# Windowed attention and a mixture of adapters: token order restored by the exp's write, the residual added outside TensorE

## The chip, the cores and the metric

The kernel runs on one core of a Trainium2 chip. The metric is the device time of one execution in microseconds (us). The profile shows the core's engines side by side: PE (TensorE, the matrix engine; PEld is its loading of weights), DVE (VectorE), ACT (ScalarE), POOL (GpSimd) and SP (SyncE, which here only issues DMA transfers). SBUF is the on-chip working memory, PSUM the memory that TensorE writes its products to.

## The reference

The first part is attention with a symmetric window of 32 positions, for 8 batches, 8 heads, 576 tokens and a head size of 64. The second part adds to each token a mixture of two of eight adapters of rank 16; both results are summed.

```python
scores = q @ k.T / sqrt(64)             # masked to |i - j| <= 32
attn = softmax(scores); x = attn @ v    # x becomes [4608 tokens, 512]
logits = x @ w_gate                     # 8 experts
top 2 of the logits, w = softmax over these two
delta = sum over the two of w * ((x @ A[e]) @ B[e])
out = x + delta                         # float32
```

The last line is what the change touches: `x` is the residual.

## The kernel before

**Attention.** q and k come in as 9 tiles (t = 0 to 8) of 128 rows, cast from float32 to float16 by DMA transfers that GpSimd issues (`load`, L397). TensorE transposes them (`trans_full`, L482; `trans`, L496 for tile 0), VectorE copies q out of PSUM to `qT` (L505) and ScalarE copies k to `kT`, permuted (L507). A row of a tile holds 16 tokens, so the 128 columns of a score block stand in the order (h, r, s), with two halves h, 16 places r within a row and 4 rows s. The natural order of the tokens is (h, s, r). `score` (L552 writes the mask with matmuls, L564 the scores) fills a PSUM tile `W`, and `expo` (L572) on ScalarE writes the exponentials as float16 into `PT`. 36 such steps run in all. v comes in through 256-byte rows on SyncE's queue (L404), and GpSimd casts it into `vbd` (L462). `pv` (L615; L643 for the last batch) multiplies `PT` with `vbd`, which has a column of ones for the softmax's sum, and VectorE divides (L628, L629; L654, L656) and writes `xs`, the attention's output x in float16.

**Adapters.** For each batch b, five groups g of 128 tokens: TensorE transposes x (`moe_xT`, L708), VectorE copies it out (L713), TensorE multiplies by the adapters' A and the gate (`moe_zl`, L726), the gate is worked out by small operations (`gate1`, `gate_e`, `gate2`, `gate3`, L748 to L769), the gated z is transposed back (`moe_zT`, L776) and copied out by ScalarE (`moe_ez`, L781). This copy also puts the tokens into natural order. `moe_pd` then makes two matmuls for each group into the same PSUM tile: z times B (L794), and x times a permuted identity `po_` (L796), which both adds the residual and brings it into natural order. ScalarE copies the sum to `ob` (`moe_eo`, L803) and SyncE's queue stores it (`moe_st`, L809 and L814). The five groups of a batch are handled in three steps j: groups 0 and 1, groups 2 and 3, group 4. The last batch (`FINE`, `GM`) runs through its gates step by step rather than in one piece.

**The order of the work.** Each piece of work is a task with an engine, an assumed duration, a due time, its predecessors and the buffers that it takes and gives back. `Planner.run` plays these through and so fixes, at build time, one order for each engine. `LEAN` holds an offset of the due time for each kind of task. Each engine executes its instructions in that order and waits in place where an input or a buffer is missing. The pools that matter here are PSUM (`W`, four tiles of 1024 float32, or eight halves `H`), `xs` (4), `ob` (7), `vraw` (5) and `raw` (3 each for q and k). The stores of batch 0 and 1 are planned behind the loads of v for batch 6 and 7.

Of the kernel before, what the change touches and what calls it, by code (L numbers as in the profile page):

```python
# [10 lines left out]
F16 = mybir.dt.float16  # L11
# [12 lines left out]
class Planner:  # L24
# [3 lines left out]
    LAT = 0.1  # L28
    PELAT = 0.26
    STICK = 0.3  # L30
    LEAN = {"cv": 219.41, "cvb": 272.89, "cw": -85.24, "cz": 71.26, "ek": 86.6,
            "eo": 453.57, "eoz": 19.28, "eq": 36.82, "ex": -18.16, "exx": -411.27,
            "exxz": 157.95, "ez": -28.43, "ezz": -32.76, "g1": -34.69, "g1z": 30.3,
            "g2": 61.29, "g2z": -68.02, "g3": -26.85, "g3z": 51.71, "ge": -5.86,
            "gez": -29.31, "ident": 1.61, "ld": -29.04, "ldw": 40.85, "lv": 308.15,
            "mask": 0.64, "nm": 38.08, "nmg": -75.15, "pad": 22.65, "pd": 378.9,
            "pdz": -55.48, "perm": -12.35, "pv": -58.89, "pvg": 96.18, "sc": 366.94,
            "st": 7.28, "stz": -11.9, "tr": -62.44, "wm": 304.62, "xT": -482.21,
            "xTz": 2.47, "zT": 16.38, "zTz": -100.13, "zero": 16.41, "zl": 329.66}
    SWITCH = 0.095  # L40
    BOOT = {"POOL": 1.3, "SP": 0.8, "ACT": 2.1, "DVE": 0.9, "PE": 0.8}
    ROT = 5
    LINE = 128
# [172 lines left out]
def kernel(  # L216
# [31 lines left out]
    QW = NI + 2 * PADQ  # L248
    BI = NP * SL
    SPLIT = (0,)  # L250
    GM = (B - 1,)
    FINE = (B - 1,)
    GATE = {t: [f"cv{t - 2}.0.0"] for t in range(3, NTI)}
# [27 lines left out]
    H = [W[i // 2][:, 512 * (i % 2):512 * (i % 2) + 512] for i in range(2 * NW)]  # L281

    ident = const.tile([128, 128], F16, name="ident")
    po_ = const.tile([128, 128], F16, name="po_")
    mask = const.tile([128, 2, RR, 4], F16, name="mask")
    WA_sb = const.tile([128, NP, ER + E], F16, name="WA")
    B_sb = const.tile([128, DD], F16, name="Bsb")
# [18 lines left out]
    def slot(p, key):  # L306
        return place[p, key]

    def wslot(key):
        return slot("W", key) // 2  # L310
# [27 lines left out]
    def c_ident():  # L338
        make_identity(nc, ident)

    def c_perm():
        nc.gpsimd.tensor_copy(
            out=po_.rearrange("p (h s r) -> p h s r", h=2, s=4),
            in_=ident.rearrange("p (h r s) -> p h s r", h=2, s=4))

    def c_mask():
        nc.gpsimd.memset(mask, 0.0)
        for h in range(2):
# [29 lines left out]
    if PACE:  # L378
        P.add("pace", "SP", 0.1, -20, c_pace, [PACE])
    P.add("ident", "POOL", 0.6, -22, c_ident, ["ld0.0.0"], lat=0.3)  # L380
    P.add("perm", "POOL", 0.3, 0, c_perm, ["ident"])
    P.add("mask", "POOL", 2.6, -21, c_mask, ["ld0.0.1"], lat=0.3)
    P.add("pad", "DVE", 0.3, -10, c_pad)
    for i in range(NVB):
# [184 lines left out]
                        start=False, stop=(i == 3))  # L569

    def expo(t):
        nc.scalar.activation(out=PTs[slot("PT", t)].rearrange("p e i c -> p (e i c)"),  # L572
                             in_=W[wslot(("s", t))],
                             func=AF.Exp, scale=1.0 / float(D) ** 0.5)

    def blocks(t):
# [125 lines left out]
    def moe_xT(b, j):  # L702
        x = xs[slot("xs", b)]
        tp = H16[slot("H", ("x", b, j))]
        for m, g in enumerate(GG[j]):
            for c in range(NP):
                o = 512 * m + 128 * c
                nc.tensor.matmul(out=tp[:, o:o + 128], lhsT=x[:, g].rearrange("p (k c) -> p c k", c=4)[:, c],  # L708
                                 rhs=ident, is_transpose=True, start=True, stop=True)
# [61 lines left out]
    def moe_zT(b, k, g0, g1):  # L771
        zs = zss[b % 2].rearrange("p g e r -> p g (e r)")
        tp = H16[slot("H", ("y", b, k))]
        for g in range(g0, g1):
            o = 128 * (g - g0)
            nc.tensor.matmul(out=tp[:, o:o + 128], lhsT=zs[:, g],  # L776
                             rhs=ident, is_transpose=True, start=True, stop=True)

    def moe_ez(b, k, g0, g1):
        tp = H16[slot("H", ("y", b, k))][:, 0:128 * (g1 - g0)]  # L780
        nc.scalar.copy(  # L781
            out=zTs[b % 2][:, g0:g1].rearrange("p g (h s r) -> p (g h) s r", h=2, s=4),
            in_=tp.rearrange("p (g r s) -> p g s r", r=RR, s=4))

    def pdt(b, j):
        key = ("d", b, j)
        t = H[slot("H", key)] if len(GG[j]) == 1 else W[wslot(key)]
        return t.rearrange("p (i c) -> p i c", c=DD)

    def moe_pd(b, j):  # L790
        pd = pdt(b, j)
        x = xs[slot("xs", b)]
        for i, g in enumerate(GG[j]):
            nc.tensor.matmul(out=pd[:, i], lhsT=zTs[b % 2][:, g], rhs=B_sb,  # L794
                             start=True, stop=False)
            nc.tensor.matmul(out=pd[:, i], lhsT=po_,  # L796
                             rhs=x[:, g],
                             start=False, stop=True)

    def moe_eo(b, j):  # L800
        n = len(GG[j])
        pd = pdt(b, j)
        nc.scalar.copy(out=obs[slot("ob", (b, j))][:, 0:n], in_=pd[:, 0:n])  # L803

    def moe_st(b, j):
        ob = obs[slot("ob", (b, j))]
# [9 lines left out]
    for b in range(B):  # L816
        d0 = 4 * b + 4.6
        fine = b in FINE
        z_ = "z" if fine else ""
        old = b >= 2  # L820
        chunks = [(g[0], g[-1] + 1) for g in GG] if fine else [(0, NG)]
        kold = range(len(GG)) if b - 2 in FINE else range(1)
        for j in range(3):
            n = len(GG[j])
            P.add(f"xT{z_}{b}.{j}", "PE", 0.225 * n, d0 + 0.1 * j, lambda b=b, j=j: moe_xT(b, j),
                  ([f"nmg{b}.{g}" for g in GG[j]] if b in GM else [f"nm{u}" for u in range(4 * b, 4 * b + 4)])
                  + ([f"zl{b - 2}.{k_}" for k_ in kold] if old else []),
                  take=[("H", ("x", b, j))], mode="full", ni=4 * n)
            P.add(f"exx{z_}{b}.{j}", "DVE", 0.15 + 0.27 * n, d0 + 0.1 * j - 0.5, lambda b=b, j=j: moe_ex(b, j),
                  [f"xT{z_}{b}.{j}"], drop=[("H", ("x", b, j))])  # L830
        for k_, (g0, g1) in enumerate(chunks):
            n = g1 - g0
            arg = (b, k_, g0, g1)
            zb = ("W" if n > 2 else "H", ("z", b, k_))
            zn = f"{z_}{b}.{k_}"
            P.add(f"zl{b}.{k_}", "PE", 0.24 * n, d0 + 0.5, lambda arg=arg: moe_zl(*arg),
                  ([f"exx{z_}{b}.{k_}"] if fine else [f"exx{b}.{j}" for j in range(3)]) + ["cw"],
                  take=[zb], mode="full", ni=4 * n)
            if not fine:
                P.add(f"cz{zn}", "ACT", 0.75, d0 - 1, lambda arg=arg: copy_z(*arg), [f"zl{b}.{k_}"]  # L840
                      + ([f"g3{b - 2}.{j}" for j in kold] if old else []), drop=[zb])
            P.add(f"g1{zn}", "DVE", 0.45 if n > 2 else 0.37, d0 - 1, lambda arg=arg: gate1(*arg),
                  [f"zl{b}.{k_}" if fine else f"cz{zn}"]
                  + ([f"zT{b - 2}.{j}" for j in kold] if old else []))
            P.add(f"ge{zn}", "ACT", 0.22, d0 - 1, lambda arg=arg: gate_e(*arg), [f"g1{zn}"])
            P.add(f"g2{zn}", "DVE", 1.0 if n > 2 else 0.88, d0 - 1, lambda arg=arg: gate2(*arg), [f"ge{zn}"])
            P.add(f"g3{zn}", "DVE", 0.33 + 0.15 * n, d0 - 1,
                  lambda arg=arg: gate3(*arg), [f"g2{zn}"], drop=[zb] if fine else [])
            P.add(f"zT{zn}", "PE", 0.055 * n, d0 + 0.8, lambda arg=arg: moe_zT(*arg), [f"g3{zn}"],
                  take=[("H", ("y", b, k_))], mode="full", ni=n)  # L850
            P.add(f"ez{zn}", "ACT", 0.2 + 0.1 * n, d0 + 0.5, lambda arg=arg: moe_ez(*arg),
                  [f"zT{zn}"] + ([f"pd{'z' if b - 2 in FINE else ''}{b - 2}.2"] if old else []),
                  drop=[("H", ("y", b, k_))])
        for j in range(3):
            n = len(GG[j])
            k_ = j if fine else 0
            P.add(f"pd{z_}{b}.{j}", "PE", 0.43 * n, d0 + 1.2 + 0.7 * j, lambda b=b, j=j: moe_pd(b, j),
                  [f"ez{z_}{b}.{k_}", "perm"], soft=[f"pd{z_}{b}.{j - 1}"] if j else [],
                  take=[(PB[n], ("d", b, j)), ("ob", (b, j))], drop=[("xs", b)] if j == 2 else [],
                  mode="full", ni=2 * n)  # L860
            P.add(f"eo{z_}{b}.{j}", "ACT", 0.2 + 0.42 * n, d0 + 1.2 + 0.7 * j,
                  lambda b=b, j=j: moe_eo(b, j), [f"pd{z_}{b}.{j}"],
                  drop=[(PB[n], ("d", b, j))])
            P.add(f"st{z_}{b}.{j}", "SP", 0.38 * (2 if j == 0 else 1), d0, lambda b=b, j=j: moe_st(b, j),
                  [f"eo{z_}{b}.{j}"], lat=1.2,
                  soft=[f"lv{b + HOLD}.1.1"] if b + HOLD < B else [])
            P.add(f"ds{b}.{j}", "Q1", 0.7 * n, d0, None, [f"st{z_}{b}.{j}"],
                  drop=[("ob", (b, j))], lat=0.8, pkt=88.0)
# [41 lines left out]
```

The softmax here doesn't subtract the row's maximum and nothing guards it: scores larger than these inputs give would overflow.

## Time and profile before

| | |
|---|---|
| time, median of 3 runs | 147.33 us (143.87 to 149.73) |
| profiled execution | 144.49 us, span 142.6 us |
| TensorE, VectorE, ScalarE, GpSimd busy | 116.4, 94.0, 84.7, 63.7 us |
| residual matmuls (L796) | 40, 10 of them before and 30 after 98.6 us |
| input read, output written | 28.85 MB, 9.44 MB |

Busy time is the time in which an engine's record shows an instruction; a matmul's end is modelled, so that the starts of successive matmuls say more than their durations. A line of the profile names the kernel's line, the engine, the operation, what it writes and reads, the shape and the count. The releaser of a wait is the instruction that ended it.

### The profile page before, as it was taken

How to read it: one execution, taken by the hardware profiler on the slowest of the kernel's cores; microseconds unless marked ns; L12 is line 12 of the kernel's file. 1: busy time of each engine (PE TensorE's matmuls, PEld its weight loads, DVE VectorE, ACT ScalarE, POOL GpSimd, SP SyncE). 2: the span in 40 equal slices, each digit the busy share in tenths (PEclk: the TensorE clock that was granted, in tenths of full speed). 3: DMA queues.
4: the chain of work that ended last, by engine and by line, in shares of the span. 5: the costliest groups of instructions: out<-in, count | busy, mean ns of one | idle time of the engine just before them, and what ended most of it. 6: DMA issues, size and time to landing. Idle time of an engine off the chain costs nothing. (4 is left out here: it accounts for less than half of the span.)

```text
span 142.6 us, 5610 instructions
## 1 busy us (share of the span) xinstructions
PE 116.4 (82%) x2413; PEld 82.7 (58%) x2413; DVE 94.0 (66%) x288; ACT 84.7 (59%) x106; POOL 63.7 (45%) x78
## 2 busy tenths in 40 slices
PE   6459999889976949997989588998699999997720
PEld 2235476467656737675778475777458668663200
DVE  5745106366794997889996089782796399897400
ACT  3022394928323928947469938729747974876850
POOL 6996302999620599972199934218500000000000
PEclk9955599999999999999999999999999999999997
DMA  3999999999999999999999999999635045288693
GB/s 79 203 205 205 205 206 219 230 199 193 225 217 221 207 251 170 219 220 212 198 228 141 210 262 230 309 229 277 219 132 203 11 151 185 95 272 290 232 339 103
DMA packets 49001, 29.22 MB, mean 205 GB/s; under 512 B 39632, under 2 KB 39632, under 8 KB 48976
## 3 DMA queue, kind: packets, MB, share of 16 engines
q1 hardware_dynamic: 43824, 19.42, 52.5%
q0 software_dynamic: 5152, 9.44, 36.9%
q8 instruction: 19, 0.31, 0.8%
q14 instruction: 6, 0.05, 0.1%
HBM read 28.85 MB, written 9.44 MB: 269 GB/s over the span
## 5 line engine op out<-in xcount | busy, mean ns | idle before, releaser
L462 POOL TENSOR_SCALAR_AFFINE_SELECT vbd<-vraw 64x1152 f16<-64x1152 f32 x32 | 40.4, 1267 | 35.5 <-DMA vraw<-in_v_dram 29.4
L572 ACT ACTIVATE PT<-W 128x1024 f16<-128x1024 f32 x36 | 34.9, 1032 | 10.9 <-PE W L564 10.7
L629 DVE TENSOR_TENSOR xs<-W,rc 128x384 f16<-128x384 f32 (+1 forms) x56 | 27.5, 491 | 1.9
L803 ACT COPY ob<-W 128x1024 f32<-128x1024 f32 (+1 forms) x24 | 21.0, 874 | 8.3 <-PE W L796 6.2
L507 ACT COPY kT<-W 128x1024 f16<-128x1024 f16 x16 | 16.0, 1018 | 6.0 <-PE W L482 3.8
L615 PE MATMUL W<-vbd,PT 128*64 128x130 f16 x504 | 18.0, 221 | 1.8 <-ACT PT L572 0.8
L505 DVE COPY qT<-W 128x1024 f16<-128x1024 f16 x16 | 10.7, 684 | 13.2 <-PE W L482 10.8
L615 PEld LDWEIGHTS <-PT 128*64 128x64 f16 x504 | 15.5, 110 | 5.8 <-issue 2.5
L482 PE MATMUL W<-ident,raw 128*64 128x128 f16 x512 | 17.8, 220 | 1.3 <-DVE xT L713 0.5
L482 PEld LDWEIGHTS <-raw 128*64 128x64 f16 x512 | 15.3, 110 | 5.6 <-issue 4.8
L628 DVE RECIPROCAL rc<-W 128x6 f32<-128x6 f32 (+1 forms) x56 | 10.1, 180 | 11.8 <-PE W L615 11.1
L564 PE MATMUL W<-qT,kT 64*64 64x128 f16 x576 | 16.1, 226 | 1.5 <-issue 1.5
L794 PE MATMUL W<-Bsb,zT 128*128 128x512 f16 x40 | 15.2, 381 | 2.4 <-ACT zT L781 1.5
L564 PEld LDWEIGHTS <-kT 64*64 64x64 f16 x576 | 13.8, 111 | 5.6 <-issue 2.4
L552 PE MATMUL W<-mask,ident 64*64 64x512 f16 x144 | 15.2, 409 | 0.7 <-DVE xs L629 0.6
L326 PE MATMUL W<-xs 128*128 128x512 f16 x37 | 13.5, 467 | 2.8 <-DVE xs L331 1.3
L796 PE MATMUL W<-xs,po__115 128*128 128x512 f16 x40 | 15.2, 379 | 0.0
L713 DVE COPY xT<-W 128x1024 f16<-128x1024 f16 (+1 forms) x24 | 13.3, 593 | 2.1 <-PE W L708 1.5
L726 PE MATMUL W<-WA,xT 128*128 128x136 f16 x160 | 11.5, 223 | 1.9 <-issue 1.6
L739 ACT COPY zl<-W 128x680 f32<-128x680 f32 x7 | 5.1, 727 | 12.0 <-PE W L726 12.0
L708 PE MATMUL W<-ident,xs 128*128 128x128 f16 x160 | 10.7, 219 | 1.5 <-DVE qT L505 1.2
L726 PEld LDWEIGHTS <-xT 128*128 128x128 f16 x160 | 9.8, 98 | 3.4 <-issue 2.4
(51 smaller groups left out, 122.2 us busy)
## 6 DMA issues: line engine op xcount, KB each, us to landing
vraw<-in_v_dram SPq DMA_DIRECT2D x32, 288.0 KB, 9.6
out_dram<-ob SPq DMA_DIRECT2D x8, 512.0 KB, 4.1
out_dram<-ob SPq DMA_DIRECT2D x16, 192.0 KB, 3.5
out_dram<-ob SPq DMA_DIRECT2D x8, 256.0 KB, 2.7
raw<-in_k_dram POOLq DMA_DIRECT2D x4, 256.0 KB, 7.5
raw<-in_q_dram POOLq DMA_DIRECT2D x4, 256.0 KB, 9.0
raw<-in_k_dram POOLq DMA_DIRECT2D x2, 448.0 KB, 8.9
raw<-in_q_dram POOLq DMA_DIRECT2D x2, 448.0 KB, 10.8
```

The lines of the kernel that those rows point to most:

```text
L462: nc.gpsimd.affine_select(out=vbt(b, e)[p, :, c:c + D], in_=vraw[slot("vr", (b, e))][p], compare_op=ALU.is_ge, fill=0.0, base=1, channel_m ...
L482: nc.tensor.matmul(out=tp[64 * hh:64 * hh + 64, 128 * (r % 8):128 * (r % 8) + 128], lhsT=src[:, hh, D * r:D * r + D], rhs=ident, is_transp ...
L507: nc.scalar.copy(out=kT[slot("kT", t)][:, :, 8 * h:8 * h + 8], in_=tp.rearrange("p r i -> p i r"))
L552: nc.tensor.matmul(out=ps[o0:o0 + 64, e], lhsT=ident[p0:p0 + 64, p0:p0 + 64], rhs=bcast(mask[p0:p0 + 64].rearrange("p h r s -> p (h r s)") ...
L564: nc.tensor.matmul(out=ps[o0:o0 + 64, e, i], lhsT=kT[slot("kT", g // 32)][p0:p0 + 64, c1:c1 + 4].rearrange("p s r -> p (s r)"), rhs=qT[p0: ...
L572: nc.scalar.activation(out=PTs[slot("PT", t)].rearrange("p e i c -> p (e i c)"), in_=W[wslot(("s", t))], func=AF.Exp, scale=1.0 / float(D) ...
L615: nc.tensor.matmul(out=po[o0:o0 + 64, GO[g]:GO[g] + 2 * VD], lhsT=PTs[slot("PT", s // 4)][:, e, s % 4, 64 * (1 - j):64 * (1 - j) + 64], rh ...
L629: nc.vector.tensor_tensor(out=x[:, g0:g1], in0=po[:, :, :, 0:D], in1=bcast(rc[:, g0:g1], 3, D), op=ALU.mult)
L726: nc.tensor.matmul(out=pz[:, g - g0, 0:ER + E], lhsT=xT[b % 2][:, g, c, :], rhs=WA_sb[:, c, :], start=(c == 0), stop=(c == NP - 1))
L794: nc.tensor.matmul(out=pd[:, i], lhsT=zTs[b % 2][:, g], rhs=B_sb, start=True, stop=False)
L796: nc.tensor.matmul(out=pd[:, i], lhsT=po_, rhs=x[:, g], start=False, stop=True)
L803: nc.scalar.copy(out=obs[slot("ob", (b, j))][:, 0:n], in_=pd[:, 0:n])
```

## The change

It has two parts and a new plan.

First, the token order is restored earlier. `expo` writes `PT` with s and r exchanged, so that `pv` puts its rows out in natural order, and all of x, z and the output stay in it. The copy in `moe_ez` becomes a plain one and the permuted identity `po_` is dropped.

Second, the residual is added elsewhere. `RES` names the steps (b, j) without a residual matmul: all steps of batches 0 to 5, and step 2 of batches 6 and 7. In steps 0 and 1 of batches 0 to 5 ScalarE copies z times B to `ob` as before, and GpSimd then adds `xs` to it in place. In the steps with j = 2 VectorE reads PSUM and `xs` and writes the sum to `ob`; ScalarE's copy is left out. Steps 0 and 1 of batches 6 and 7 keep the matmul, with the plain identity. The purpose is to take work from TensorE.

```diff
+    RES = {(b, j): "DVE" if j == 2 else "POOL" for b in range(6) for j in range(3)} | {(6, 2): "DVE", (7, 2): "DVE"}
...
     def expo(t):
-        nc.scalar.activation(out=PTs[slot("PT", t)].rearrange("p e i c -> p (e i c)"),
-                             in_=W[wslot(("s", t))],
+        nc.scalar.activation(out=PTs[slot("PT", t)].rearrange("p e i (h s r) -> p (e i h) s r", h=2, s=4),
+                             in_=W[wslot(("s", t))].rearrange("p (x r s) -> p x s r", r=RR, s=4),
                              func=AF.Exp, scale=1.0 / float(D) ** 0.5)
...
         nc.scalar.copy(
-            out=zTs[b % 2][:, g0:g1].rearrange("p g (h s r) -> p (g h) s r", h=2, s=4),
-            in_=tp.rearrange("p (g r s) -> p g s r", r=RR, s=4))
+            out=zTs[b % 2][:, g0:g1].rearrange("p g t -> p (g t)"), in_=tp)
...
             nc.tensor.matmul(out=pd[:, i], lhsT=zTs[b % 2][:, g], rhs=B_sb,
-                             start=True, stop=False)
-            nc.tensor.matmul(out=pd[:, i], lhsT=po_,
+                             start=True, stop=(b, j) in RES)
+            if (b, j) in RES:
+                continue
+            nc.tensor.matmul(out=pd[:, i], lhsT=ident,
                              rhs=x[:, g],
                              start=False, stop=True)
...
+    def moe_res(b, j):
+        n = len(GG[j])
+        ob = obs[slot("ob", (b, j))][:, 0:n]
+        x = xs[slot("xs", b)][:, GG[j][0]:GG[j][0] + n]
+        if RES[b, j] == "POOL":
+            nc.gpsimd.tensor_tensor(out=ob, in0=ob, in1=x, op=ALU.add)
+        else:
+            nc.vector.tensor_tensor(out=ob, in0=pdt(b, j)[:, 0:n], in1=x, op=ALU.add)
```

The planner gets the new task `rs` with assumed durations of 2.1 us on GpSimd and 0.64 us on VectorE, gives `xs` back after the last add of a batch, has a new set of `LEAN` offsets and somewhat longer assumed durations for transposes and for a change of TensorE's mode. So the order of nearly every engine's queue is a new one: among other things GpSimd builds `ident` and the mask ahead of the q load of tile 1, and six of its twelve adds stand among the casts of v and the loads of q and k.

## The prediction

> **What bounds the kernel now.** I began with the page's first part, busy time by engine (share of the 142.6 us span, instructions).
>
> ```profile
> PE 116.4 (82%) x2413; PEld 82.7 (58%) x2413; DVE 94.0 (66%) x288; ACT 84.7 (59%) x106; POOL 63.7 (45%) x78
> ```
>
> TensorE is the fullest, but an average over the span hides stages, so next came the stages: start to end, PE, PEld, DVE, ACT and POOL busy (with instructions), granted clock, DMA share, GB/s.
>
> ```profile
> 41.00:60.00 19.00, 15.31 (x384) 11.95 (x381) 15.61 (x43) 11.42 (x15) 13.01 (x14) 1.00 1.09 213
> 60.00:80.00 20.00, 18.00 (x411) 14.29 (x412) 16.32 (x46) 13.85 (x18) 13.14 (x15) 1.00 1.04 201
> 80.00:98.60 18.60, 15.00 (x382) 12.07 (x383) 12.30 (x39) 12.08 (x15) 8.34 (x8) 1.00 1.09 252
> 98.60:131.00 32.40, 29.84 (x522) 21.07 (x517) 26.07 (x93) 23.63 (x33) 2.78 (x3) 1.00 0.52 179
> 131.00:137.00 6.00, 4.14 (x20) 1.35 (x18) 1.91 (x11) 4.53 (x10) 0.00 (x0) 1.00 0.72 245
> ```
>
> 98.60 is where the last q tile is transposed. Until then the DMA share is 1.04 to 1.09: the input transfers keep the DMA engines full. After it they have room (0.52), and TensorE is busy 29.84 of 32.40 us (92%), VectorE 26.07 (80%). Over 41 to 137 us TensorE sums to 82.30 of 96 (86%) and VectorE to 72.20 (75%).
>
> The waits say whether the full DMA holds the engines up. Three rows (waiter, releaser: total us, times, longest), the first over the whole span, the others after 98.6:
>
> ```profile
> POOL vbd L462 <- DMA vraw<-in_v_dram: 29.4, 8, 8.5
> DVE rc L628 <- PE W L615: 5.3, 3, 2.5
> PE W L794 <- ACT zT L781: 1.5, 4, 0.6
> ```
>
> GpSimd waits for v. After 98.6 VectorE waits for TensorE in its largest row, TensorE for nobody more than 1.5 us in one row; over the whole span the only DMA waits among TensorE's are in the first 13 us. So TensorE's order is the bound, VectorE close behind; transfers run ahead of use by a few us (k and q of tile 8 are issued at 80.79, land after 8.4 and 12.1 us, and are transposed at 94.96 and 98.60: about 5 us to spare). The chain that ended last holds only three pieces (the last two copies) and tells nothing more.
>
> Then the costs: page groups, then rows of the grouping by shape, then TensorE's timeline over one `moe_pd`.
>
> ```profile
> L462 POOL TENSOR_SCALAR_AFFINE_SELECT vbd<-vraw 64x1152 f16<-64x1152 f32 x32 | 40.4, 1267 | 35.5 <-DMA vraw<-in_v_dram 29.4
> L572 ACT ACTIVATE PT<-W 128x1024 f16<-128x1024 f32 x36 | 34.9, 1032 | 10.9 <-PE W L564 10.7
> L507 ACT COPY kT<-W 128x1024 f16<-128x1024 f16 x16 | 16.0, 1018 | 6.0 <-PE W L482 3.8
> ```
>
> ```profile
> L803 ACT COPY ob<-W 128x512 f32<-128x512 f32 x8 | 4.7, 590 | 1.4 <-ACT ob L803 0.7 <-DVE xT L713 0.7
> L629 DVE TENSOR_TENSOR xs<-W,rc 128x384 f16<-128x384 f32 x28 | 15.6, 557 | 1.0
> L629 DVE TENSOR_TENSOR xs<-W,rc 128x256 f16<-128x256 f32 x28 | 11.9, 424 | 1.0
> ```
>
> ```profile
> 86.24 0.38 PE L794 MATMUL W<-Bsb,zT 128*128 128x512 f16 x1 [0.59 <-DVE xs L629]
> 86.45 0.38 PE L796 MATMUL W<-xs,po__115 128*128 128x512 f16 x1
> 86.67 0.38 PE L794 MATMUL W<-Bsb,zT 128*128 128x512 f16 x1
> 86.88 0.38 PE L796 MATMUL W<-xs,po__115 128*128 128x512 f16 x1
> ```
>
> The reader should see that a 512-column matmul shows 0.38 us in the record, but the next starts 0.21 to 0.22 later: 0.216 is what removing one saves, not 0.38.
>
> **What the Trainium skill says.** "TensorE: Matmul & The Clock Gate", Back-to-back issue gap, gives an isolated gap of N/2.4 GHz + 2.5 ns, 215.8 ns at 512; the trace agrees (0.64 us over three). "GPSIMD Engine Reference", 3.1, measures a two-input add of 2048 fp32 per partition at 4497 ns; no operation in the trace is of this kind. "SBUF — State Buffer", Who interferes with whom: a VectorE instruction with at most one SBUF input, outside its two-port modes, does not contend with GpSimd, one with two does. No run here shows either yet.
>
> **The change, part by part.**
>
> Removed: 32 of 40 residual matmuls (all 30 of batches 0 to 5, one each of 6 and 7): 32 x 0.216 = 6.9 us of TensorE, 22 of them or more after 98.6, where it is the bound (30 of the 40 stand there now). ScalarE loses the eight 512-wide copies, 8 x 0.59 = 4.7 us. The permutation tile costs 0.29 us once on GpSimd: nothing.
>
> Added on VectorE: eight adds, PSUM plus xs, 512 wide. From the two L629 rows, (557 - 424)/128 = 1.04 ns per element, so 424 + 256 x 1.04 = 0.69 us; x 8 = 5.5 us. One SBUF input, so no lock.
>
> Added on GpSimd: twelve in-place adds of 1024 per partition. Not in the trace. Lower bound, the L462 rate with one input: 1267/1152 = 1.10 ns, 1.13 us each; by the skill half of 4497, 2.25 us; if VectorE's two-input gating locks it out or the mixed types are slow, perhaps twice that. I take 2.25: 27 us in all. POOL waits 29.4 us for v, but its queue is in order. In the compiled order, six adds stand among the v casts and q/k loads, six after the last cast. The fourth and fifth adds stand ahead of two casts and of tile 8's loads, queued behind them: 2 x 2.25 = 4.5 us moves their issue from 80.8 to some 85.3, which uses up the 5 us spare but not more. The adds of batch 3 stand behind the batch 7 casts, and VectorE's first batch 7 normalisation reuses their xs buffer and waits for them.
>
> Moved at no cost: the exp writes PT permuted and reads PSUM with a stride. L507 already reads permuted and takes 1018 ns against the 1032 of L572 for as many elements; a strided read is therefore priced at zero, and the zT copy loses its permutation. Upper bound if it isn't so: 36 x a few tenths on ScalarE, which has 30 us of room in 41 to 137.
>
> The schedule is replanned. In the compiled order, work on TensorE from the last q transposes to the end, by the spacings of the trace (0.216 per matmul of 512 columns, 0.45 per score group, 1.17 per 36 of PV, 1.12 and 1.2 per 20 of L708 and L726): before 31.0 us, after 22.4. So 6.9 is gone or nearly, and some 1.5 net (two score groups, 18 PV, one set of transposes, less five matmuls) stands ahead of that point. VectorE after its last qT copy: 26.3 us before, 25.8 after: it gains adds in the tail, but a gate and its copies (3.7 us) moved ahead, beside three adds. VectorE becomes the fuller engine of the tail.
>
> **The sum.** Over 41 to 137 us TensorE falls to 82.3 - 6.9 = 75.4 and VectorE rises to 72.2 + 5.5 = 77.7. Kept as dense as TensorE is now (86%), VectorE needs 90.6 us instead of 96: 5.4 less. From the tail: the last qT copy ends at 103.45, the last gate product at 135.44, 32.0 us with 26.3 of work. Later by the 1.5 us, then 25.8 plus 3.5 of idle that the serial last batch keeps, ends at 134.3: 1.1 less. With no shift, 2.6. The last copy on ScalarE (0.59 behind another one) becomes a VectorE add behind nothing, some 0.6 less. I take 4.0, between 1.7 and 5.4 and nearer the upper because VectorE is seen idle for TensorE in the tail. From the median 147.33: 143.3.
>
> **The rivals.** Full relief: TensorE alone sets the end, all 6.9 comes through: 140.4. For it: it is the fullest engine in every stage; against it: VectorE's sum above. VectorE takes over: 1.1 saved, 146.2; for it, the counted tail and its small serial gate operations; against, its 5.3 us of waits for PV. GpSimd is late, and the change is slower: say 4.5 us an add. Five of the six early adds stand ahead of tile 8's loads, 22.5 us; half of the 20.5 us of waits for v in 41 to 98.6 may take some of it (the adds wait for ScalarE's copies where they stand, so not all), and 5 are spare: 7.3 us late, less the 4.0 of the forecast: 3.3 slower, 150.6. For it: tile 8's spare is used up already at 2.25, and the batch 3 adds gate the last normalisations; against: GpSimd is 45% busy now, and the new VectorE adds do not lock it out.
>
> **How the numbers follow.** Forecast case 45%, VectorE takes over 25%, full relief 12%, GpSimd late 18%. The runs of before spread from 143.87 to 149.73, so a gain of 4.0 (2.7%) will not always read as over 2%: faster takes full relief, four fifths of the forecast case and a fifth of the VectorE case, 0.53; slower takes the GpSimd case, 0.18 and 0.01 for spread; the rest 0.28 is within 2%. The range runs from 138.5, full relief with a good run, to 149.5, which leaves out the worse part of the GpSimd case.
>
> **What would show it.** L796 falls to 8, TensorE busy to about 109; VectorE to about 99.5 with eight adds near 0.69; twelve GpSimd adds near 2.25; the exp still near 1032. After the last q transposes, TensorE below 85% and VectorE above 85% would show the bound changing hands. A GpSimd add over 3 us, waits of TensorE or VectorE for GpSimd or for raw loads, or an exp above 1.2 us would make the forecast wrong.

## The result and the profile after

The changed kernel takes 169.19 us (median of 4 runs, 167.51 to 172.32), the kernel before 147.37 us beside it (143.87 to 149.73). The ratio is 1.158, with a 95% interval of 1.128 to 1.187: slower by 22 us, where 143.3 was forecast and the range ended at 149.5. Executions of one kernel come in a faster and a slower kind: medians here are over all of them, ratios over the faster ones alone. In the profiled execution the span is 165.9 us instead of 142.6, and the mean granted TensorE clock 0.877 instead of 0.958.

First the busy time by engine, in the changed kernel:

```profile
PE 118.8 (72%) x2381; PEld 87.8 (53%) x2381; DVE 122.3 (74%) x296; ACT 80.8 (49%) x98; POOL 89.3 (54%) x89
```

The 32 matmuls are gone (2413 to 2381), and GpSimd has risen by 25.6 us (63.7 to 89.3), as much as its adds take (25.4). VectorE is the line to stop at: it was to go from 94.0 to 99.5 and shows 122.3, with eight instructions more. Some 23 us were added to instructions that the diff doesn't touch.

Then the stages. 109.30 us is the start of the last q transposes, which was 98.60 before, so the changed kernel is 10.7 us late there and loses another 12.6 after it (56.6 us to the end instead of 44.0). The columns are as in the prediction; the last line sums them over 41 to 163 us.

```profile
41.00:60.00 19.00, 15.96 (x396) 12.84 (x395) 16.45 (x44) 12.94 (x16) 12.82 (x12) 1.00 1.02 202
60.00:80.00 20.00, 14.50 (x328) 12.35 (x328) 17.21 (x42) 10.38 (x13) 16.11 (x15) 0.91 1.03 204
80.00:109.30 29.30, 22.10 (x515) 18.42 (x512) 24.37 (x55) 16.91 (x21) 15.04 (x13) 0.88 0.94 217
109.30:157.00 47.70, 30.04 (x427) 21.61 (x421) 38.87 (x85) 19.10 (x26) 19.27 (x11) 0.79 0.28 96
157.00:163.00 6.00, 2.27 (x12) 0.70 (x9) 3.18 (x13) 2.70 (x6) 0.00 (x0) 0.97 0.85 297
sum 122.00, PE 84.86 PEld 65.91 DVE 100.08 ACT 62.03 POOL 63.24; mean PE 16.97 PEld 13.18 DVE 20.02 ACT 12.41 POOL 12.65
```

In the stage after the last transposes VectorE is busy for 38.87 us with 85 instructions; the stage of before had 93 instructions in 26.07. TensorE is idle for 17.7 of the 47.7 us, and the clock that it is granted falls to 0.79. VectorE over 41 to 163 us is 100.08 where the prediction's sum has 77.7.

Which instructions grew shows when the groups are kept apart by shape. The rows are picked out; the columns after the bar are busy us and mean ns of one, then the idle time ahead of them:

```profile
L764 DVE TENSOR_TENSOR zs<-zl,gate 128x640 f16<-128x640 f32 x7 | 9.1, 1294 | 0.2
L755 DVE TENSOR_TENSOR lm<-e,m 128x40 f32<-128x40 f32 x7 | 8.9, 1270 | 0.2
L752 DVE SCALAR_TENSOR_TENSOR lm<-t,e 128x40 f32<-128x40 f32 x7 | 7.6, 1092 | 0.3 <-ACT e L748 0.3
L808 DVE TENSOR_TENSOR ob<-W,xs 128x512 f32<-128x512 f32 x8 | 5.5, 684 | 2.8 <-PE W L788 1.4 <-ACT zT L776 1.0 <-PE W L721 0.4
L756 DVE TENSOR_SCALAR s<-m 128x5 f32<-128x5 f32 x7 | 5.1, 726 | 0.0
L763 DVE TENSOR_TENSOR gate<-lm,s 128x40 f32<-128x40 f32 x7 | 4.1, 582 | 0.1
L744 DVE TENSOR_TENSOR t<-zl,m 128x40 f32<-128x40 f32 x7 | 3.7, 522 | 0.2
...
L754 DVE TENSOR_REDUCE m<-lm 128x5 f32<-128x40 f32 x7 | 1.4, 196 | 0.2
```

Apart from L808, the new add, these are the operations of the gate. In the kernel before, the first three and the fifth were:

```profile
L769 DVE TENSOR_TENSOR zs<-zl,gate 128x640 f16<-128x640 f32 x7 | 5.8, 825 | 0.2
L760 DVE TENSOR_TENSOR lm<-e,m 128x40 f32<-128x40 f32 x7 | 2.2, 309 | 0.2
L757 DVE SCALAR_TENSOR_TENSOR lm<-t,e 128x40 f32<-128x40 f32 x7 | 1.3, 191 | 0.5 <-ACT e L753 0.5
L761 DVE TENSOR_SCALAR s<-m 128x5 f32<-128x5 f32 x7 | 1.1, 164 | 0.0
```

Two more grew: `gate` (L763) from 376 to 582, `t` (L744) from 316 to 522. The excess, seven of each: 3.3 + 6.7 + 6.3 + 3.9 + 1.4 + 1.4 = 23.0 us, which with the 5.5 us of L808 makes the whole rise of VectorE. The reduction at L754 has not moved (197 before).

What they meet is seen when VectorE and GpSimd are laid over one another. First VectorE, then GpSimd (start, duration, instructions):

```profile
126.89 1.85 DVE L752 SCALAR_TENSOR_TENSOR lm<-t,e 128x40 f32<-128x40 f32 x1
128.77 0.20 DVE L754 TENSOR_REDUCE m<-lm 128x5 f32<-128x40 f32 x1
129.00 1.82 DVE L755 TENSOR_TENSOR lm<-e,m 128x40 f32<-128x40 f32 x1
130.74 2.12 DVE L756 TENSOR_SCALAR s<-m 128x5 f32<-128x5 f32 x1
```

```profile
126.53 6.30 POOL L806 TENSOR_TENSOR ob<-ob,xs 128x1024 f32<-128x1024 f32 x3 [10.41 <-issue]
```

Three adds run from 126.53 to 132.83, so one ends near 128.6 and one near 130.7. L752 ends as the first add does, L755 as the second does, L756 as the third does. Each wants 0.2 us and waits out one add. The reduction in between, with one input, takes its usual 0.20.

Not all of the excess is the adds'. With every gate operation set beside what GpSimd runs meanwhile, ten long ones stand beside adds and are 17.6 us above their shortest time together; ten more stand beside the casts of v (1.27 us each) and are 9.5 us above it. Before, the casts met six, for 4.0 us (17.6 + 9.5 - 4.0 = 23.1, the same rise). All of what `zs` lost and all of what `gate` lost is beside casts, as here (VectorE, then four casts of GpSimd in a row):

```profile
113.64 1.20 DVE L763 TENSOR_TENSOR gate<-lm,s 128x40 f32<-128x40 f32 x1
114.87 1.92 DVE L764 TENSOR_TENSOR zs<-zl,gate 128x640 f16<-128x640 f32 x1
```

```profile
110.87 5.25 POOL L457 TENSOR_SCALAR_AFFINE_SELECT vbd<-vraw 64x1152 f16<-64x1152 f32 x4
```

The waits over the whole span (waiter, releaser: total us, times, longest) and the chain that ended last (shares of the span, by engine and by line) show who pays:

```profile
POOL vbd L457 <- DMA vraw<-in_v_dram: 18.7, 4, 9.3
PEld L771 <- DVE zs L764: 17.2, 8, 6.6
```

```profile
DVE 34%; PE 30%; DMA 18%; issue 7%; POOL 5%; ACT 3%; SPq 1%; ACTq 0%; DVEq 0%; POOLq 0%
DMA vraw<-in_v_dram 13%; PE W L721 6%; PE W L610 6%; DVE lm L755 5%; DMA raw<-in_k_dram 5%; PE W L477 4%; DVE xT L708 4%; DVE lm L752 4%; DVE xs L624 4%; POOL vbd L457 3%; PE W L788 3%; DVE zs L764 3%; PE W L771 3%; PE W L703 3%; DVE s L756 3%
```

The weight loads of the transposes of z wait 17.2 us for the gate's product; before, they waited 2.0. The gate is serial, each of its operations needs the one before, and TensorE's queue is in order behind them. Four gate lines (L755, L752, L764, L756) alone make 15% of the chain, some 25 us.

### The profile page after: what moved, and what is told of

Its sections match the earlier page's. It is cut to its first block, busy times and chain, and to the rows that moved or that the text cites. A ratio compares the mean times of both kernels' runs of the same rounds, so it can differ in the third digit from the quotient of the medians.

```text
span 165.9 us, 5564 instructions
## 1 busy us (share of the span) xinstructions
PE 118.8 (72%) x2381; PEld 87.8 (53%) x2381; DVE 122.3 (74%) x296; ACT 80.8 (49%) x98; POOL 89.3 (54%) x89
## 4 chain that ended last, share of the span: by engine, by line
DVE 34%; PE 30%; DMA 18%; issue 7%; POOL 5%; ACT 3%; SPq 1%; ACTq 0%; DVEq 0%; POOLq 0%
DMA vraw<-in_v_dram 13%; PE W L721 6%; PE W L610 6%; DVE lm L755 5%; DMA raw<-in_k_dram 5%; PE W L477 4%; DVE xT L708 4%; DVE lm L752 4%; DVE xs L624 4%; POOL vbd L457 3%; PE W L788 3%; DVE zs L764 3%; PE W L771 3%; PE W L703 3%; DVE s L756 3%
## 5 line engine op out<-in xcount | busy, mean ns | idle before, releaser
L806 POOL TENSOR_TENSOR ob<-ob,xs 128x1024 f32<-128x1024 f32 x12 | 25.4, 2131 | 37.1 <-issue 22.2
L477 PE MATMUL W<-ident,raw 128*64 128x128 f16 x512 | 18.9, 231 | 5.9 <-DMA raw<-in_k_dram 2.3
L721 PE MATMUL W<-WA,xT 128*128 128x136 f16 x160 | 14.9, 263 | 9.9 <-DVE xT L708 9.9
L477 PEld LDWEIGHTS <-raw 128*64 128x64 f16 x512 | 16.5, 116 | 9.6 <-issue 9.0
L799 ACT COPY ob<-W 128x1024 f32<-128x1024 f32 x16 | 15.9, 1014 | 10.0 <-DVE xs L651 3.3
L610 PE MATMUL W<-vbd,PT 128*64 128x130 f16 x504 | 19.9, 234 | 1.1 <-POOL vbd L457 0.5
L721 PEld LDWEIGHTS <-xT 128*128 128x128 f16 x160 | 13.4, 118 | 11.6 <-DVE xT L708 10.1
L610 PEld LDWEIGHTS <-PT 128*64 128x64 f16 x504 | 17.4, 119 | 3.0 <-issue 1.1
L771 PE MATMUL W<-ident,zs 128*128 128x128 f16 x40 | 5.4, 279 | 16.7 <-DVE zs L764 9.6
L776 ACT COPY zT<-W 128x640 f16<-128x640 f16 (+2 forms) x10 | 5.9, 588 | 18.8 <-PE W L771 10.9
```

Source lines behind the costliest of these rows:

```text
L477: nc.tensor.matmul(out=tp[64 * hh:64 * hh + 64, 128 * (r % 8):128 * (r % 8) + 128], lhsT=src[:, hh, D * r:D * r + D], rhs=ident, is_transp ...
L610: nc.tensor.matmul(out=po[o0:o0 + 64, GO[g]:GO[g] + 2 * VD], lhsT=PTs[slot("PT", s // 4)][:, e, s % 4, 64 * (1 - j):64 * (1 - j) + 64], rh ...
L721: nc.tensor.matmul(out=pz[:, g - g0, 0:ER + E], lhsT=xT[b % 2][:, g, c, :], rhs=WA_sb[:, c, :], start=(c == 0), stop=(c == NP - 1))
L806: nc.gpsimd.tensor_tensor(out=ob, in0=ob, in1=x, op=ALU.add)
```

## The experiments

The theory that came out of this: a GpSimd add reads SBUF, a VectorE operation with two inputs in SBUF can't run beside it, and waits for its end. The rivals: the new order of the work costs the time (the offsets), GpSimd is simply occupied for too long and late with what is queued behind the adds, or the exp's permuted write costs. All times are medians, each with the kernel before beside it in the same runs.

### The parts one by one: order of tokens, adds on VectorE

```diff
-    RES = {(b, j): "DVE" if j == 2 else "POOL" for b in range(6) for j in range(3)} | {(6, 2): "DVE", (7, 2): "DVE"}
+    RES = {}
```

> The changed kernel with the table of moved residuals empty: token order restored by the exp, all 40 residual matmuls back on TensorE, the new due-time offsets kept, the order planned anew. Lock theory (GpSimd's adds hold VectorE's gate operations up): no adds, so VectorE busy falls from 122 to about 94 us and the time to that of the kernel before, 147 us within 2 per cent. Queue theory (adds delay casts and loads in GpSimd's order): the same. Plan theory (the new offsets make a bad order, adds or not): stays above 155 us. Exp theory (permuted write is slow): above 150 us with exps over 1.1 us.

```diff
-    RES = {(b, j): "DVE" if j == 2 else "POOL" for b in range(6) for j in range(3)} | {(6, 2): "DVE", (7, 2): "DVE"}
+    RES = {(b, 2): "DVE" for b in range(8)}
```

> Only the eight 512-wide adds on VectorE moved, the twelve GpSimd adds left out and their 24 residual matmuls back on TensorE. Lock theory: no GpSimd adds, so the gate operations are back near 0.2 us each; VectorE about 94 + 5.5 = 99.5 us, TensorE 8 x 0.216 = 1.7 us less, time 144 to 149 us. Queue theory: the same. If the VectorE adds themselves were the fault: above 155 us.

Order alone: 150.55 us against 148.48 (ratio 1.029, 1.006 to 1.052). With the eight VectorE adds and no GpSimd add: 149.52 (1.026, 1.006 to 1.046). So without GpSimd's adds nearly all of the 22 us is gone. What stays, 2 to 3%, may be the permuted exp or the new offsets. Two more kernels, with the offsets and the `SWITCH` value of before, tell these apart:

```diff
...
-            "eo": 597.91, "eoz": 61.8, "eq": -10.53, "ex": -27.46, "exx": -525.49,
+            "eo": 453.57, "eoz": 19.28, "eq": 36.82, "ex": -18.16, "exx": -411.27,
...
-    SWITCH = 0.14
+    SWITCH = 0.095
...
-    RES = {(b, j): "DVE" if j == 2 else "POOL" for b in range(6) for j in range(3)} | {(6, 2): "DVE", (7, 2): "DVE"}
+    RES = {}
```

> Token order by the exp's write alone, no residual moved, offsets of the kernel before. If the 1.2 per cent that the run with eight VectorE adds and the old offsets lost come from the adds: 145 to 147 us, like the kernel before. If they come from the order or from luck in how the plan meets the casts: 148 us or more, with VectorE above 97 us.

The other has the same offsets and `RES = {(b, 2): "DVE" for b in range(8)}`:

> Token order and only the eight VectorE adds, planned with the offsets of the kernel before. If the 2 to 3 per cent that the two runs without GpSimd adds lost against the kernel before come from the new offsets: 143 to 147 us, no slower than before. If they come from VectorE's eight adds or the exp's write: 149 us or more again.

Order alone with the old offsets: 147.37 us (144.06 to 148.48) against 146.38 (143.72 to 148.39); the runs give no interval, and the ranges lie over one another. The exp takes 1029 ns there and 1028 with the new offsets (1032 before): the permuted write is free. That points to the new offsets, used without the GpSimd adds, for the 2 to 3%; without an interval it isn't more than that. The eight VectorE adds with the old offsets: 149.18 against 146.5, ratio 1.012 (1.007 to 1.018). They gain nothing, although they take eight matmuls from TensorE. In that kernel `t` at its L743 averages 505 ns and `lm` at its L756 513 (316 and 356 before) without any add on GpSimd; in its trace every gate operation that is too long stands beside a cast of v.

### The same occupation without the reading

Each add becomes two fills of the same tile, with the same task, duration and place in the plan; the values of these twelve steps are left out. A fill, unlike the add, has no need to wait for `xs`.

```diff
-            nc.gpsimd.tensor_tensor(out=ob, in0=ob, in1=x, op=ALU.add)
+            nc.gpsimd.memset(ob, 0.0)
+            nc.gpsimd.memset(ob, 0.0)
```

> The changed kernel, same plan and same order on every engine, but each GpSimd add replaced by two fills of the same output tile with zero: GpSimd writes and reads nothing. The output of these twelve steps is zero, so the result of steps 0 and 1 of batches 0 to 5 is left out. Lock theory, the lock being on the reads of two-input operations: gate operations back to 0.2 to 0.4 us, VectorE about 100 us, time 142 to 148 us. Queue theory: fills of about 2 us in the same places delay casts and loads all the same, the time stays at 160 to 169 us; if the fills are much shorter than the adds, somewhat less.

146.64 us (142.08 to 148.92) against 148.48 (144.01 to 149.24), no interval; level or a little faster. GpSimd by form:

```profile
L807 POOL MEMSET ob<- 128x1024 f32 x12 | 11.5, 954 | 0.7
L806 POOL MEMSET ob<- 128x1024 f32 x12 | 11.4, 951 | 18.9 <-issue 14.7 <-ACT ob L799 4.2
```

That is 22.9 us in place of 25.4, in the same order, and 22 us of time are back. The same stretch of the gate on VectorE, beside fills that run on GpSimd from 119.06 to 122.97:

```profile
119.44 0.19 DVE L752 SCALAR_TENSOR_TENSOR lm<-t,e 128x40 f32<-128x40 f32 x1
...
119.90 0.20 DVE L755 TENSOR_TENSOR lm<-e,m 128x40 f32<-128x40 f32 x1
120.02 0.16 DVE L756 TENSOR_SCALAR s<-m 128x5 f32<-128x5 f32 x1
```

What took 5.8 us beside adds (L752, L755, L756) takes 0.55 beside fills. So it is neither GpSimd's being occupied nor the order of the work: for the two-input operations it is that the adds read.

L756, with one input, is an exception. Here it falls between two fills, of which one ends at 120.03 and the next begins at 120.08. Where it starts inside a fill, it is held to the fill's end, and L757 behind it too (VectorE, then GpSimd):

```profile
85.01 0.64 DVE L756 TENSOR_SCALAR s<-m 128x5 f32<-128x5 f32 x1
85.13 0.53 DVE L757 TENSOR_TENSOR lm<-lm,e 128x40 f32<-128x40 f32 x1
```

```profile
84.67 0.95 POOL L806 MEMSET ob<- 128x1024 f32 x1 [1.40 <-ACT ob L799]
```

VectorE stands at 105.3 us; most of what is over 99.5 stands beside the casts of v, which lengthen the gate by 9.6 us here and by 9.5 in the changed kernel. So it is not the casts that cost the 22 us. The last q transposes start at 104.49, 5.9 us later than before, in a profiled execution that is itself 4.6 us longer (span 147.2); what this lateness costs by itself isn't shown.

### Shorter adds

```diff
-            nc.gpsimd.tensor_tensor(out=ob, in0=ob, in1=x, op=ALU.add)
+            for i in range(n):
+                for c in range(0, DD, 128):
+                    nc.gpsimd.tensor_tensor(out=ob[:, i, c:c + 128], in0=ob[:, i, c:c + 128],
+                                            in1=x[:, i, c:c + 128], op=ALU.add)
```

> The changed kernel with each GpSimd add cut into eight of 128 elements per partition, same plan. Lock theory: a VectorE operation waits for one piece of some 0.3 us and no longer for 2.1, so the excess of VectorE's busy time falls from 23 us to about 6 to 10 (the casts still collide), time 148 to 156 us. Queue theory: GpSimd needs as long or longer for the pieces together, time 165 us or more.

155.19 us against 148.48 (1.068, 1.040 to 1.097), and VectorE at 111.8. The 96 pieces take 451 ns each, 39.7 us in all instead of 25.4, and the time still falls by 14 us: what counts is how long a gate operation is held, not how long GpSimd works. But one wait was not of one piece. VectorE, then GpSimd:

```profile
128.07 7.72 DVE L752 SCALAR_TENSOR_TENSOR lm<-t,e 128x40 f32<-128x40 f32 x1
```

```profile
125.70 10.03 POOL L808 TENSOR_TENSOR ob<-ob,xs 128x128 f32<-128x128 f32 x26
```

L752 starts inside an unbroken row of 26 pieces and ends when the row does (135.79 against 135.73). Most other small gate operations that meet pieces take 0.3 to 0.5 us. Pieces that follow one another without a gap can thus keep VectorE out for the whole row; what decides whether it gets in between two of them, no run here shows.

### The held operations taken away, the adds kept

Five of the seven gate operations that can be held become reciprocals of one input; the gate isn't computed then.

```diff
-        nc.vector.scalar_tensor_tensor(out=lm, in0=t, scalar=0.0, in1=e,
-                                       op0=ALU.is_lt, op1=ALU.mult)
+        nc.vector.reciprocal(out=lm, in_=e)
...
-        nc.vector.tensor_tensor(out=lm, in0=e, in1=bcast(m2, 2, E), op=ALU.is_ge)
-        nc.vector.tensor_scalar(out=s, in0=m2, scalar1=1.0, scalar2=None, op0=ALU.add)
-        nc.vector.tensor_tensor(out=lm, in0=lm, in1=e, op=ALU.mult)
+        nc.vector.reciprocal(out=lm, in_=e)
+        nc.vector.reciprocal(out=s, in_=m2)
+        nc.vector.reciprocal(out=lm, in_=e)
...
-        nc.vector.tensor_tensor(out=gate, in0=lm, in1=bcast(s, 2, E), op=ALU.mult)
+        nc.vector.reciprocal(out=gate, in_=lm)
```

> The changed kernel with its GpSimd adds as they are, but five of the seven small VectorE operations of a gate (the four of two SBUF inputs in gate2 and gate3, and the add of 1) replaced by reciprocals of one input; the gate is not computed rightly. The first operation of gate1 and the product with z keep two inputs. Lock theory, seen from VectorE's side: reciprocals stay at 0.16 to 0.2 us beside an add, the excess of VectorE's busy time falls from 23 to some 5 us, time 146 to 153 us. Queue theory: GpSimd does the same work in the same places, 165 us or more.

147.03 us against 146.5, ratio 1.004 (0.9985 to 1.0094), with all twelve adds in place. Ten take 2.12 to 2.15 us; two take 2.71, each queued behind an add that a `zs` was waiting for: the `zs` ran first, so an add can be held as well. The reciprocals are dearer than I took them for, but steady (202 to 406 ns):

```profile
L756 DVE RECIPROCAL lm<-e 128x40 f32<-128x40 f32 x7 | 2.8, 403 | 0.0
```

The two operations that still have two inputs are still held: `t` averages 638 ns, `zs` 1155, with a longest of 2.2 us, and 4.9 us are still lost beside adds instead of 17.6. Together with the fills this settles it from both sides: with the adds and without the operations they hold, or with the operations and without the reading, the 22 us are not there.

### Another place for the adds in the plan

All of the changed kernel's work, with the offsets and `SWITCH` of before (the diff of the old offsets above, `RES` as in the change):

> The changed kernel, adds included, planned with the due-time offsets and the mode cost of the kernel before. Lock theory: the adds still meet the gates, though at other places, VectorE's excess 12 to 25 us, time above 155 us. Plan theory: back to 147 to 150 us.

155.62 us against 146.5 (1.052, 1.048 to 1.057): with the same adds 9 us are lost instead of 22. So the loss depends on the plan around the adds. The profiled execution is the longest of the four, 162.96 us; in it VectorE is at 116.3, 16.8 over the planned 99.5, and seven gate operations stand beside adds instead of ten. That it is the meetings with the gate that make the difference is likely, but not shown apart from the rest of the plan.

Then a token that the planner gives either to a GpSimd add or to a part of the gate, so that it plans them apart:

```diff
+    P.pool("lk", 1)
...
-            P.add(f"g2{zn}", "DVE", 1.0 if n > 2 else 0.88, d0 - 1, lambda arg=arg: gate2(*arg), [f"ge{zn}"])
+            P.add(f"g2{zn}", "DVE", 1.0 if n > 2 else 0.88, d0 - 1, lambda arg=arg: gate2(*arg), [f"ge{zn}"],
+                  take=[("lk", f"g2{zn}")], drop=[("lk", f"g2{zn}")])
...
+                      take=[("lk", ("rs", b, j))] if res == "POOL" else [],
...
```

> The changed kernel, but the planner holds a token for each GpSimd add and for each piece of a gate on VectorE, so that it never plans the two at the same time; the work and the waits on the chip are the same. Lock theory: fewer meetings as far as the chip follows the plan; VectorE's excess falls below 15 us, time 147 to 160 us. Queue theory: no change, or worse, as adds start later.

VectorE falls to 106.6, so most of the holding is gone, yet the time is 161.06 us against 146.5 (1.097, 1.093 to 1.102), where the theory had 160 at most. The plan is only a plan: the `lm` that is L752 above still averages 903 ns here. And GpSimd waits 21.1 us for ScalarE's copies ahead of its adds. Why this kernel loses 14 us with so little holding isn't settled; a plan can lose time in other ways than by the lock.

### The gate's operands in PSUM

`t`, `lm`, `m2` and z stay in spare columns of z's PSUM tile, so that no operation of the gate has two inputs in SBUF. ScalarE's copy of z is left out, and z's tile is held until the gate is done. The heart of the edit:

```diff
+    GC = {"t": (ER + E, E), "lm": (ER + 2 * E, E), "m2": (ER + 3 * E, 1)}
...
-    def gtiles(b, g0, g1, names):
-        return (gt[x][b % 2][:, g0:g1] for x in names)
+    def gtiles(b, k, g0, g1, names):
+        pz = zbank(b, k, g1 - g0)
+        for x in names:
+            if x == "m2":
+                yield pz[:, :, ER + 3 * E]
+            elif x in GC:
+                yield pz[:, :, GC[x][0]:GC[x][0] + E]
+            else:
+                yield gt[x][b % 2][:, g0:g1]
...
-                  lambda arg=arg: gate3(*arg), [f"g2{zn}"], drop=[zb] if fine else [])
+                  lambda arg=arg: gate3(*arg), [f"g2{zn}"], drop=[zb])
```

In the changed kernel:

> The changed kernel with its GpSimd adds, the gate computed in full, but with z, the shifted logits, the masked weights and the second maximum left in PSUM, in the spare columns of z's own tile, so that every VectorE operation of a gate has at most one SBUF input; ScalarE's copy of z falls away (8 x 0.73 us), and z's PSUM tile is held until the gate ends. Planned with the same offsets. Lock theory: no gate operation above 0.25 us and z's product at 0.82, VectorE near 99.5 us, time 143 to 149 us, the rest being what the longer hold of PSUM costs. Queue theory: 165 us or more.

The same edit in the kernel before:

> The kernel before with the gate in PSUM alone. Lock theory: the casts of v also meet the gates there, at 1.3 us each; VectorE's busy time falls by some 3 to 4 us, time 142 to 147 us unless the longer hold of z's PSUM tile costs more than that; then 148 to 152.

In the changed kernel, without adds on VectorE (`RES = {(b, j): "POOL" for b in range(6) for j in range(3)}`):

> The gate in PSUM and the twelve GpSimd adds, but no VectorE add: ten of the 40 residual matmuls of batches 0 to 5 and 7, and all of 6, stay on TensorE (16 in all). Lock theory: the adds are free, TensorE loses 24 x 0.216 = 5.2 us and VectorE gains nothing, 141 to 147 us. If PSUM's hold or GpSimd's queue is the next bound: no better than the run with both kinds of adds.

In the changed kernel it takes 153.86 us against 146.38 (1.051, 1.028 to 1.075), in the kernel before 155.96 (no interval), in the last form 157.45 (1.087, 1.065 to 1.109); all three are longer than the theory alone had it. VectorE in the changed kernel, by form:

```profile
L768 DVE TENSOR_TENSOR zs<-W,gate 128x640 f16<-128x640 f32 x7 | 5.8, 824 | 0.2
L759 DVE TENSOR_TENSOR W<-e,W 128x40 f32<-128x40 f32 x7 | 1.4, 204 | 0.2
L756 DVE SCALAR_TENSOR_TENSOR W<-W,e 128x40 f32<-128x40 f32 x7 | 1.4, 203 | 3.8 <-ACT e L752 3.8
```

Every operation of the gate takes its bare time again, beside twelve adds of 2132 ns that read SBUF; twenty of these operations begin while an add runs, and none is longer for it. VectorE is at 96.8 us. Read as a square: with the gate in SBUF the change takes 147.4 to 169.2; with the gate in PSUM, 156.0 to 153.9, within the spread of these runs (152.4 to 158.0 and 151.2 to 157.8). The edit has a price of its own, 146.4 to 156.0 in the kernel before. There ScalarE's exp waits 17.4 us for the scores instead of 10.7; that z's tile, held longer, keeps PSUM from the scores would explain it but was not tested by itself. Why the last form is slower than the one with VectorE adds isn't settled either. None of the twelve kernels is faster than the kernel before by more than its runs can tell.

## Why the prediction was wrong, step by step

**What held.** TensorE loses its 32 matmuls, L792 has 8 left. The VectorE add takes 684 ns (0.69 forecast), the GpSimd add 2131 (2.25, from the Trainium skill, "GPSIMD Engine Reference", 3.1: 5% too high). The exp's permuted write is free. VectorE is the fuller engine at the end, here mostly by held time (38.87 us against TensorE's 30.04), but narrowly also beside fills (27.46 against 26.33 from 104.5 to 138 us). Tile 8's transposes come later, though by 10.7 us where 1.5 were counted.

**The step that failed** is the cost of "Added on GpSimd", where it came to the lock. It asked what VectorE's gating could do to an add ("if VectorE's two-input gating locks it out") and doubled the add for its upper bound. It never asked what an add does to the gate. The adds were not held (2110 to 2147 ns); the gate was. Hence the term of the sum "VectorE rises to 72.2 + 5.5 = 77.7" lacked 22.4 us and was measured at 100.1; 17.6 us of it stand beside the adds themselves, the rest is mostly more meetings with casts in the new order. "One SBUF input, so no lock" was true of the new VectorE adds (674 to 692 ns) and said nothing of the seven gate operations, six of which grew.

The Trainium skill has the rule, in "SBUF — State Buffer", Who interferes with whom, of which I used one half: a VectorE instruction with two SBUF inputs contends with a GpSimd instruction that reads SBUF, not with one that only writes; the shared pair goes to whoever comes first, for the whole instruction, and "the other fully blocks". The runs agree with each part: two-input operations of 0.2 us take up to 2.1 beside adds, 0.2 beside fills and 0.2 with one operand in PSUM, and the reductions are untouched. L756 has one input; by the same page a `tensor_scalar` may use both ports and then contends with GpSimd, reading or not, which fits its 2.12 us beside an add and its 0.61 and 0.64 beside fills.

The trace of before had shown it, too, in the part that means hide. There the gate's `lm` has a median of 201 ns and a longest of 959 at L760, a longest of 1295 at L762: casts of 1.27 us, met now and then. Against the bare times of the run with the gate in PSUM the four means at L749, L760, L762 and L768 are 109 + 105 + 148 + 181 ns too long, seven of each: 3.8 us over the whole kernel, which passes for noise; the adds are longer, and seven of the twelve run after 108 us.

**"Kept as dense as TensorE is now (86%)"** failed with it. VectorE's share of its stretch rose from 75 to 82%, but with time held, in which the serial gate kept TensorE waiting (17.2 us at L771). TensorE then also ran slower, and is busy for 118.8 us with 32 matmuls less, where about 109 was expected:

```profile
152.28 0.63 PE L788 MATMUL W<-Bsb,zT 128*128 128x512 f16 x1
152.70 0.63 PE L792 MATMUL W<-xs,ident 128*128 128x512 f16 x1
153.13 0.63 PE L788 MATMUL W<-Bsb,zT 128*128 128x512 f16 x1
153.56 0.63 PE L792 MATMUL W<-xs,ident 128*128 128x512 f16 x1
```

Between 152.28 and 155.48 us its 512-column matmuls start 0.42 to 0.43 us apart (but for one place, where others stand between), where 0.216 was used. The Trainium skill, "TensorE: Matmul & The Clock Gate", Wait — 56ns, not 53.3ns?, gives 426.7 ns for the array's cold state, and the trace agrees. How much of the 22 us is this clock and how much the waiting itself is open.

**The rival on the slower side**, GpSimd late with loads and casts, gave 150.6 and was not the cause: with fills GpSimd is occupied for nearly as long in the same order, at 146.6.

**The gain itself** was also too high. Where the adds hold little or nothing, the times are 146.64 against 148.48 and 147.03 against 146.5, not 4 us faster. The casts, which still hold the gate, and the reciprocals' own cost blur this, so I don't put a number on what the removed matmuls are worth.

## What to carry to other kernels

Before giving GpSimd an operation that reads SBUF, list the VectorE operations with two SBUF inputs, and each `tensor_scalar` from SBUF to SBUF, that can run beside it, and allow for at least one whole GpSimd instruction on each; a 0.2 us operation in a serial chain took up to 2.1. Look at the longest durations of small operations, not their means: a few at the length of another engine's instruction show the lock before the change. Moving one operand to PSUM freed the operations here, but has to be priced too: in the kernel before, that edit cost 9.6 us, for a reason that no run isolates.

## What was not expected of the hardware

- A fill, which only writes, leaves the two-input operations alone but holds the `tensor_scalar` of 5 elements (0.61 and 0.64 us instead of 0.16).
- Splitting doesn't always bound the wait: one VectorE operation waited 7.72 us through a row of 451 ns pieces.
- A GpSimd add of 128 elements takes 451 ns and one of 1024 takes 2131: by these two an estimate of about 0.2 us fixed and 1.9 ns per element. A fill of 1024 takes 0.95 us.
- A reciprocal of 40 elements takes 0.40 us on VectorE, twice a two-input operation of the same size (0.20).
